# K and V as 8 KB rows, and P and dS turned by VectorE blocks, in a one-core attention and MLP gradient kernel

## The chip, the core and the metric

The kernel runs on one core of one Trainium2 chip. Its time is the device time of one execution in microseconds. The engines are named as the profile names them: PE is TensorE (PEld its weight loads), DVE is VectorE, ACT is ScalarE, POOL is GpSimd, SP is SyncE. Transfers issued by SP run on queue q1, those issued by POOL on queue q0; both are served by the same 16 DMA engines of the core.

## The reference

One decode step of a transformer block (attention and a gated MLP side by side on a normalised input) and its gradients. Cut to what matters:

```
xn = layernorm(x)                                  # x: [4, 1, 512]
q  = (xn @ wq) -> [4 batches, 32 heads, 128]
k, v = last 1024 of 4096 cache rows, 8 key heads, each shared by 4 query heads
p  = softmax(q k^T / sqrt(128));  o = p v
out = x + o @ wo + (gelu(xn @ w_gate) * (xn @ w_up)) @ w_down
results: out and the gradients by x, k_cache, v_cache, wq, wo, w_gate, w_up, w_down
```

All tensors are bf16. The gradients by k_cache and v_cache have the full shape [4, 8, 4096, 128]; the first 3072 rows of each head are zeros and are written as zeros. With them, each execution writes 81 MB and reads 31 MB.

## The kernel before

The kernel has four stages. The MLP stage (to about 60 us in the profiled execution) computes the MLP forward and backward and the weight gradients dW_down, dW_up and dW_gate. A short stage then forms q and the gradient of the attention output (`do_ps`), spread over masks (`bd`, `rows`, `dyBD`). The attention stage runs over the 4 batches b. The end stage forms out, dx, dW_o and dW_q.

In each batch, `scores(0, b)` forms S from q and K, and `scores(1, b)` forms dP from the output gradient and V. Each does four DVE transposes of 128 x 1024 uint32 into a scratch tile `scr` (two buffers) and 8 PE products per transpose, with 32 weight columns and 256 moving columns. `softmax` gives P; `turned` turns P so that keys lie on partitions; `odq(0, b)` multiplies P by V; `spread` and `dvdk(0, b)` form dV; `softmax_d` gives dS; then `turned`, `odq(1, b)` (dq, reads K) and `dvdk(1, b)` (dK). A `dvdk` makes 16 PSUM banks (`kv_ps`), each copied by `evac` into one of four staging tiles `stg`, and stores two tiles of 1 MB.

K and V of a batch are 2 MB each. A tile holds 128 partitions x 8 heads x 8 key rows x 128; partition m has key rows 8m to 8m+7 of every head, so that a run in memory is 2 KB. `load_kv` loads it as two transfers of 1 MB. V has one buffer (`va`), K two (`ka`, `kb`). K of batch 0 is issued by SP, all other K and V by POOL, as are all result stores (`result`). POOL issues in one order with its copies and memsets.

The zeros are written by SP as 32 transfers of 1.5 MB from `ztile` with rows of 12 KB from every second partition (`zeros`). At most three are in flight, and most are tied to an event: two or more follow the landing of each load of K or V, the last ones follow a softmax, an `odq` or an eviction. They fill the transfers' time between loads and stores.

A planner orders the instructions of each engine other than SP from costs; `evac` picks ACT or DVE by running totals (`load`). What sets the order of POOL's transfers before is this planner.

In `turned`, 32 PE products with P (or dS) as weights and a 32-column selection `selp` as the moving operand write one PSUM bank, and one copy evicts it:

```
for j in range(J):
    for a, q in enumerate(quad):
        mm(ps[q, j, :], src[:, j * Q:(j + 1) * Q], selp[:, a].rearrange("p c r -> p (c r)"), pos=(0, Q * a))
pT = att.tile([P, J, Q], BF16, name="pT", tag=f"pT{k}")
evac(pT[:], ps[:], NJ)
```

Of the kernel before, what the change touches and what calls it, by code (L numbers as in the profile page):

```python
# [8 lines left out]
ACT = mybir.ActivationFunctionType  # L9
# [9 lines left out]
def kernel(  # L19
# [71 lines left out]
    def t32(out, in_, n):  # L91
        load["dve"] += (130 + n) / 0.96
        nc.vector.transpose(out=out, in_=in_)  # L93
# [17 lines left out]

    def result(out, in_):
        return store(nc.gpsimd, out, in_, "rest", ["zeros", "rest"], single_packet=True)

    def mm(out, lhsT, rhs, first=True, last=True, pos=None):
        kw = {} if pos is None else {"tile_position": pos}
        nc.tensor.matmul(out, lhsT=lhsT, rhs=rhs, start=first, stop=last, **kw)  # L117
# [42 lines left out]
    def mask(name, n, in_):  # L160
# [10 lines left out]
    omt = const.tile([P, NQ, 2], FP32, name="omt")  # L171
    TT(out=omt[:], in0=gmask[:].rearrange("p (c g) -> p c g", g=2), in1=bm[:].unsqueeze(2).broadcast_to([P, NQ, 2]),
       op=ALU.mult)
    om = mask("om", 2, omt[:].rearrange("p c g -> p g c"))
    oms = const.tile([P, 2], FP32, name="oms")
    TS(out=oms[:], in0=om[:], scalar1=scale, scalar2=None, op0=ALU.mult)
# [7 lines left out]
    selp = const.tile([P, 4, NQ, 8], BF16, name="selp")  # L184
    for a in range(4):
        TS(out=selp[:, a], in0=rs2[:, :, 0, :], scalar1=amask[:, a:a + 1], scalar2=None, op0=ALU.mult)
# [26 lines left out]
    dyBD = const.tile([P, NPB, 2, P], BF16, name="dyBD")  # L213
    nc.gpsimd.memset(dyBD[:], 0.0)
# [12 lines left out]
    def load_kv(b, k, pool, tag, eng, **kw):  # L227
        d_, src = ((k_t, A_k_cache), (v_t, A_v_cache))[k]
        tl = pool.tile([P, G, J, Dh], BF16, name=tag, tag=tag)
        for hf in range(2):  # L230
            hs = slice(hf * G // 2, (hf + 1) * G // 2)
            with tc.high_priority():
                d = eng.dma_start(out=tl[:, hs].rearrange("p g j d -> p g (j d)"),  # L233
                                  in_=src[b, hs, K0:Sk, :].rearrange("g (m j) d -> m g (j d)", j=J), **kw)
# [25 lines left out]
    if True:  # L260
# [85 lines left out]
        for wi, (wsb, dh, og) in enumerate(((wu_sb, dhu, out_7), (wg_sb, dhg, out_6))):  # L346
# [26 lines left out]
            for h in range(2):  # L373
# [7 lines left out]
                result(dwg_v[h], stg[:, 0:2 * F])  # L381
# [3 lines left out]
    with tc.tile_pool(name="mid", bufs=1, reuse_waits="tile") as mid:  # L385
# [4 lines left out]
        with tc.tile_pool(name="att", bufs=1, reuse_waits="tile") as att:  # L390
            zeros(2, load_kv(0, 1, att, "va", nc.gpsimd, single_packet=True))
            zeros(3, load_kv(1, 0, att, "kb", nc.gpsimd, single_packet=True))

# [4 lines left out]
            for k in range(2):  # L398
                bd.append([])
                for u in range(2):  # L400
                    t_ = att.tile([P, DPB, NQ, 2, 2, Q], BF16, name=f"bd{k}{u}")
                    nc.gpsimd.memset(t_[:], 0.0)
                    bd[k].append(t_)
# [65 lines left out]

            spread_rows(1, get_d)  # L470
# [9 lines left out]

            def scores(k, b):
# [4 lines left out]
                for g2 in range(2):  # L486
                    for e in range(2):
                        sc = scratch()
                        t32(sc[:].rearrange("p (c j m) -> p c j m", c=NQ, j=J), src[:, g2:G:2, :, e * Q:(e + 1) * Q], 1024)
                        sb = sc[:].bitcast(BF16).rearrange("p (c n r) -> p c r n", c=NQ, r=2)  # L490
# [15 lines left out]
            def turned(src, k):  # L506

                ps = bank("pT_ps", "x", (P, J, Q))
                for j in range(J):
                    for a, q in enumerate(quad):  # L510
                        mm(ps[q, j, :], src[:, j * Q:(j + 1) * Q], selp[:, a].rearrange("p c r -> p (c r)"), pos=(0, Q * a))
                pT = att.tile([P, J, Q], BF16, name="pT", tag=f"pT{k}")
                evac(pT[:], ps[:], NJ)
# [32 lines left out]
            def softmax_d(P_f, dP):  # L546
# [9 lines left out]
                STT(out=dS_b[:], in0=dP, scalar=cc[:, 0:1], in1=P_f[:], op0=ALU.subtract, op1=ALU.mult)  # L556
                load["dve"] += 1200
                return dS_b

            def dvdk(k, b, sp, r_):  # L560
# [4 lines left out]
                for j in range(0, J, 2):  # L565
                    ps = [bank("kv_ps", "w", (P, 2, 2, Dh)) for _ in range(NQ)]
                    for u in range(2):
                        for c, q in enumerate(quad):
                            mm(ps[c][:, u].rearrange("p g d -> p (g d)"), sp[q, j + u].rearrange("p a m -> p (a m)"),
# [208 lines left out]
```

## Time and profile before

| what | value |
|---|---|
| median of 3 runs | 282.73 us (281.98 to 283.4) |
| the profiled execution | 282.91 us, its span 280.8 us |
| busy in the span | PE 67%, DVE 58%, ACT 44%, POOL 21% |
| queue q1 (SP) | 66.46 MB, 57.0% of 16 engines |
| queue q0 (POOL) | 45.35 MB, 41.5% of 16 engines |
| moved | 112.21 MB, mean 400 GB/s |
| granted PE clock | mean 0.581 |

The span runs from the first to the last instruction; 2.1 us of the time lie outside it. The share of a queue is the time that its packets took, over 16 engines for the span. The attention stage begins at about 76 us and its last store is issued at 241.8 us.

### The profile page before, as it was taken

To read this page: it belongs to the slowest core of one execution; us is meant where nothing else is said; L and a number is where in the kernel's file an instruction comes from. 1 tells how busy PE (TensorE), PEld (TensorE's weight loads), DVE (VectorE), ACT (ScalarE), POOL (GpSimd) and SP (SyncE) were. 2 spreads that over 40 slices of the span, in tenths; PEclk is the share of its full clock that TensorE was granted. 3 is DMA by queue.
4 is the path that set the end of the run, shared out by engine and by line. 5 is a ranking of instruction groups with operands and counts; after the bars stand their busy time and mean duration, and the time that the engine had idled before them with its cause. 6 is when DMAs were issued, how large, how long until landed. Compare 5 with 4: busy or idle time off the path is not lost.

```text
span 280.8 us, 4407 instructions
## 1 busy us (share of the span) xinstructions
PE 187.0 (67%) x1733; PEld 76.1 (27%) x1733; DVE 162.9 (58%) x309; ACT 124.3 (44%) x245; POOL 60.2 (21%) x135
## 2 busy tenths in 40 slices
PE   0318899859444899659956642963357998955870
PEld 0102354233122623224321321321034232511210
DVE  2879656898796525545128350474496104397870
ACT  1133764730100569634824402722441768445870
POOL 8500110169083314130040060020020020201110
PEclk9975955558955556655555555555555555685555
DMA  7999999999999999999999999999999999999995
GB/s 246 427 443 443 388 396 420 425 426 411 389 427 434 420 356 403 308 373 415 424 412 407 421 427 409 371 428 427 436 373 418 415 408 402 390 411 386 414 412 242
DMA packets 17027, 112.21 MB, mean 400 GB/s; under 512 B 1384, under 2 KB 1648, under 8 KB 11376
## 3 DMA queue, kind: packets, MB, share of 16 engines
q1 hardware_dynamic: 6688, 66.46, 57.0%
q0 software_dynamic: 10176, 45.35, 41.5%
q8 instruction: 13, 0.21, 0.3%
q10 hardware_dynamic: 144, 0.13, 0.1%
q14 instruction: 6, 0.05, 0.0%
HBM read 30.93 MB, written 81.01 MB: 399 GB/s over the span
## 4 chain that ended last, share of the span: by engine, by line
PE 25%; DMA 24%; DVE 13%; issue 4%; ACT 4%; POOL 1%; POOLq 0%; DVEq 0%; ACTq 0%
DMA out_dram<-stg 16%; PE kv_ps L117 9%; DVE scr L93 6%; DMA ka<-in_A_k_cache_dram 5%; PE sc_ps L117 3%; ACT stg L88 3%; DMA kb<-in_A_k_cache_dram 3%; PE od_ps L117 3%; PE ok_ps L117 2%; PE ob_ps L117 2%; DVE stg L89 2%; DVE wq_sb L93 2%; PE dxq_ps L117 2%; PE dwq_ps L117 1%; PE dwo_ps L117 1%
## 5 line engine op out<-in xcount | busy, mean ns | idle before, releaser
L88 ACT CAST stg<-kv_ps 128x512 bf16<-128x512 f32 x118 | 63.7, 606 | 56.1 <-DMA out_dram<-stg 28.1
L106 POOL DMA_DIRECT2D out_dram<-stg x30 | 19.7, 659 | 146.3 <-ACT stg L88 96.1
L117 PE MATMUL sc_ps<-scr,bd 128*32 128x256 bf16 x256 | 24.2, 395 | 21.2 <-DVE scr L93 17.9
L117 PE MATMUL kv_ps<-dm,spr 32*128 32x256 bf16 x128 | 28.8, 400 | 6.7 <-ACT stg L88 5.1
L117 PE MATMUL kv_ps<-qm,spr 32*128 32x256 bf16 x128 | 24.9, 385 | 11.0 <-ACT stg L88 10.5
L93 DVE STREAM_TRANSPOSE scr<-va 128x1024 uint32<-128x1024 uint32 x16 | 18.8, 1217 | 10.9 <-DMA va<-in_A_v_cache_dram 10.9
L117 PEld LDWEIGHTS <-spr 32*128 32x128 bf16 x256 | 12.3, 102 | 46.3 <-issue 42.0
L117 PEld LDWEIGHTS <-bd 128*32 128x32 bf16 x256 | 8.1, 107 | 33.4 <-issue 32.7
L88 ACT CAST stg<-dwg_ps 128x448 bf16<-128x448 f32 x26 | 12.7, 552 | 6.7 <-PE dwg_ps L117 5.8
L88 ACT CAST stg<-dwo_ps 128x512 bf16<-128x512 f32 x18 | 10.0, 588 | 10.1 <-PE dwo_ps L117 9.9
L117 PE MATMUL dwo_ps<-dy_b,oSP 32*128 32x512 bf16 x32 | 9.0, 516 | 6.6 <-ACT stg L88 5.2
L89 DVE CAST stg<-kv_ps 128x512 bf16<-128x512 f32 x10 | 6.6, 679 | 11.8 <-DMA out_dram<-stg 6.3
L93 DVE STREAM_TRANSPOSE scr<-ka 128x1024 uint32<-128x1024 uint32 x8 | 9.6, 1227 | 5.4 <-DMA ka<-in_A_k_cache_dram 3.3
L93 DVE STREAM_TRANSPOSE scr<-kb 128x1024 uint32<-128x1024 uint32 x8 | 9.8, 1232 | 5.0 <-DMA kb<-in_A_k_cache_dram 4.4
L233 POOL DMA_DIRECT2D va<-in_A_v_cache_dram x8 | 6.0, 756 | 30.9 <-PE od_ps L117 27.1
L588 DVE SCALAR_TENSOR_TENSOR odt<-od_ps,oms,odt 128x128 f32<-128x128 f32 x4 | 1.4, 340 | 18.0 <-ACT odt L587 18.0
L117 PE MATMUL do_ps<-scr,dyBD 128*128 128x512 bf16 x32 | 10.1, 454 | 2.3 <-DVE scr L93 2.1
L117 PE MATMUL dwq_ps<-dqSP,xn_b 32*128 32x512 bf16 x32 | 10.6, 587 | 1.1 <-ACT stg L88 0.4
L89 DVE CAST stg<-dwq_ps 128x512 bf16<-128x512 f32 x15 | 9.9, 688 | 1.8 <-PE dwq_ps L117 1.6
L117 PEld LDWEIGHTS <-pT 128*32 128x32 bf16 x256 | 9.2, 140 | 5.2 <-ACT pT L88 2.3
L88 ACT CAST stg<-dwq_ps 128x512 bf16<-128x512 f32 x17 | 9.6, 586 | 1.6 <-PE dwq_ps L117 0.9
L89 DVE CAST stg<-dwo_ps 128x512 bf16<-128x512 f32 x14 | 9.2, 679 | 1.9 <-PE dwo_ps L117 1.6
(196 smaller groups left out, 321.1 us busy)
## 6 DMA issues: line engine op xcount, KB each, us to landing
out_dram<-ztile SPq DMA_DIRECT2D x32, 1536.0 KB, 12.2
out_dram<-stg POOLq DMA_DIRECT2D x24, 1024.0 KB, 10.7
va<-in_A_v_cache_dram POOLq DMA_DIRECT2D x8, 1024.0 KB, 15.0
out_dram<-stg POOLq DMA_DIRECT2D x6, 896.0 KB, 10.8
wq_sb<-in_A_wq_dram SPq DMA_DIRECT2D x1, 4096.0 KB, 24.0
wo_sb<-in_A_wo_dram SPq DMA_DIRECT2D x1, 4096.0 KB, 34.2
kb<-in_A_k_cache_dram POOLq DMA_DIRECT2D x4, 1024.0 KB, 19.4
ka<-in_A_k_cache_dram SPq DMA_DIRECT2D x2, 1024.0 KB, 42.2
```

The costliest lines, as they stand in the source:

```text
L88: return nc.scalar.copy(out=out, in_=in_)
L89: return nc.vector.tensor_copy(out=out, in_=in_)
L93: nc.vector.transpose(out=out, in_=in_)
L106: d = eng.dma_start(out=out, in_=in_, **kw)
L117: nc.tensor.matmul(out, lhsT=lhsT, rhs=rhs, start=first, stop=last, **kw)
L233: d = eng.dma_start(out=tl[:, hs].rearrange("p g j d -> p g (j d)"), in_=src[b, hs, K0:Sk, :].rearrange("g (m j) d -> m g (j d)", j=J), **kw)
L588: done = STT(out=t_[:], in0=ps[:, 1, :], scalar=mk[:, 1:2], in1=t_[:], op0=ALU.mult, op1=ALU.add)
```

## The change

Four things change together.

1. K and V tiles become [128, 2, 32, 128]: partition 4m+c holds key rows 32m to 32m+31 of heads 2c and 2c+1, so that a run in memory is 8 KB. A load is four transfers of 512 KB, one for each c, each writing every fourth partition. In `scores`, the DVE transposes read this layout, and the products' moving operand picks its 256 columns out of `scr` with steps of 1 KB, 16 B and 128 B, where it had a step of 4 B.
2. `turned` transposes P or dS by 32 x 32 blocks on DVE, does 16 PE products with a constant selection (`sel4`) as weights and 64 moving columns, and evicts the bank in four parts, each with a per-partition mask (`pmask`) and all 256 columns, two on DVE and two on ACT. `odq` then has, as weights, slices of this tile with zeros where the partition is of another c.
3. POOL's transfers get a fixed order, that of the program (`in_order`). The last store of the MLP stage is written after the first loads of V and K. `later` adds order without a wait: the first products of `dvdk` come after the last of `odq`, and the transposes of wq are placed in the last batch.
4. The two masks of dP (`bd[1]`) lie in the memory of `dyBD`, which is cleared by a POOL memset after `do_ps`.

```
     def load_kv(b, k, pool, tag, eng, **kw):
         d_, src = ((k_t, A_k_cache), (v_t, A_v_cache))[k]
-        tl = pool.tile([P, G, J, Dh], BF16, name=tag, tag=tag)
-        for hf in range(2):
-            hs = slice(hf * G // 2, (hf + 1) * G // 2)
+        tl = pool.tile([P, 2, Q, Dh], BF16, name=tag, tag=tag)
+        row = tl[:].ap[0][0]
+        for c in range(NQ):
             with tc.high_priority():
-                d = eng.dma_start(out=tl[:, hs].rearrange("p g j d -> p g (j d)"),
-                                  in_=src[b, hs, K0:Sk, :].rearrange("g (m j) d -> m g (j d)", j=J), **kw)
+                d = eng.dma_start(out=bass.AP(tensor=tl.tensor, offset=tl.offset + c * row,
+                                              ap=[[NQ * row, Q], [Q * Dh, 2], [1, Q * Dh]]),
+                                  in_=src[b, 2 * c:2 * c + 2, K0:Sk, :].rearrange("g (m j) d -> m g (j d)", j=Q), **kw)
+            if eng is nc.gpsimd:
+                in_order(d)
...
-                    t_ = att.tile([P, DPB, NQ, 2, 2, Q], BF16, name=f"bd{k}{u}")
-                    nc.gpsimd.memset(t_[:], 0.0)
-                    bd[k].append(t_)
+                    if k == 0:
+                        t_ = att.tile([P, DPB * NQ * 4 * Q], BF16, name=f"bd{u}")[:]
+                        nc.gpsimd.memset(t_, 0.0)
+                    else:
+                        t_ = dyBD_t[:, u * 1024:(u + 1) * 1024]
...
+            nc.gpsimd.memset(dyBD_t[:], 0.0)
             spread_rows(1, get_d)
...
-                        t32(sc[:].rearrange("p (c j m) -> p c j m", c=NQ, j=J), src[:, g2:G:2, :, e * Q:(e + 1) * Q], 1024)
-                        sb = sc[:].bitcast(BF16).rearrange("p (c n r) -> p c r n", c=NQ, r=2)
+                        turned_last[0] = t32(sc[:].rearrange("p (j x) -> p j x", j=Q),
+                                             src[:, g2, :, e * Q:(e + 1) * Q], 1024)
+                        sb = sc[:].bitcast(BF16).rearrange("p (h j m c r) -> p c r j m h", h=4, j=J, m=8, c=NQ)
...
-            def turned(src, k):
-
-                ps = bank("pT_ps", "x", (P, J, Q))
-                for j in range(J):
+            def turned(src):
+
+                T = att.tile([P, J, 4, 8], BF16, name="T", tag="T")
+                t32(T[:].rearrange("p j a r -> p (j a r)"), src[:], NJ)
+                ps = bank("pT_ps", "x", (P, 4, J, 8))
+                for h in range(4):
                     for a, q in enumerate(quad):
-                        mm(ps[q, j, :], src[:, j * Q:(j + 1) * Q], selp[:, a].rearrange("p c r -> p (c r)"), pos=(0, Q * a))
-                pT = att.tile([P, J, Q], BF16, name="pT", tag=f"pT{k}")
-                evac(pT[:], ps[:], NJ)
+                        mm(ps[q, h], sel4[:, h, :], T[:, :, a, :], pos=(0, Q * a))
+                pT = att.tile([P, 4, J, Q], BF16, name="pT", tag="pT")
+                pv = pT[:].rearrange("p h l (c r) -> p (h l) c r", c=NQ)
+                for c in range(NQ):
+                    in_ = ps[:].rearrange("p h l r -> p (h l) r")
+                    if c % 2:
+                        nc.scalar.activation(out=pv[:, :, c], in_=in_, func=ACT.Copy, scale=pmask[:, c:c + 1])
+                    else:
+                        TS(out=pv[:, :, c], in0=in_, scalar1=pmask[:, c:c + 1], scalar2=None, op0=ALU.mult)
```

The compiled order of the changed kernel shows where the pieces fall. In the first batch, DVE's order after the softmax is: the third transpose of the next batch's K, the block transpose `T`, the four `spread` operations, the first masked eviction, the product with dP (`Gt`), the fourth transpose of K, the second masked eviction. PE does 23 score products of the next batch ahead of the 16 of `turned`, and 9 more between these and the `od_ps` products. POOL's order from then on is: V of the next batch (4 transfers), two dV stores, K (4), two dK stores, and so on.

## The prediction

> **What bounds the kernel now.** I read the page's slices first, then the queues' totals, then the queues stretch by stretch, and last the order of the engines where the DMA row dips. First the page: span, DMA row, queues.
>
> ```profile
> span 280.8 us, 4407 instructions
> DMA  7999999999999999999999999999999999999995
> q1 hardware_dynamic: 6688, 66.46, 57.0%
> q0 software_dynamic: 10176, 45.35, 41.5%
> ```
>
> No slice but the first and last is under 90%, and the two queues' packets took 98.5% of the 16 engines' span. No compute engine is over 67%. So bytes, at their price in DMA time, set the end; the change moves the same bytes. It can win by a lower price of a byte or by filling a gap, and lose by a higher price or a new gap. Compute matters only where the transfers run dry.
>
> The price comes from the queue rows of short stretches (packets, MB, share). In order: 71 to 77 us, loads of K and V alone; 150 to 175, zeros (q1) with loads and stores (q0); 253 to 263, stores of 8 KB rows beside zeros; 265 to 274, the same alone; 85 to 95, zeros alone; 110 to 124, loads and stores of 2 KB rows together.
>
> ```profile
> q0 software_dynamic: 599, 2.31, 102.1%
> ...
> q1 hardware_dynamic: 699, 7.73, 73.0%
> q0 software_dynamic: 714, 2.76, 27.5%
> ...
> q0 software_dynamic: 315, 2.29, 56.1%
> ...
> q0 software_dynamic: 511, 3.68, 99.6%
> ...
> q1 hardware_dynamic: 384, 4.23, 99.8%
> ...
> q0 software_dynamic: 927, 3.61, 79.5%
> ```
>
> MB over share times length gives MB per us of the 16 engines. Rows of 2 KB: alone 2.31/6.13 = 0.377, beside zeros 2.76/6.88 = 0.401, in the mixed stretch 3.61/11.1 = 0.324. Rows of 8 KB: alone 3.68/8.96 = 0.411, beside zeros 2.29/5.61 = 0.408. Zeros, 12 KB rows: 4.23/9.98 = 0.424. Bytes over packets tell the grain: 3.9 KB per packet for 2 KB rows, 7.3 KB for 8 KB rows.
>
> The one gap inside the attention stage, by DMA slices of 0.2 us from 98 to 106 us, and what stands before it (VectorE, PE and POOL in order of time):
>
> ```profile
> DMA  9599896998999999998999999998563523396974
> ...
> 91.59 1.25 DVE L93 STREAM_TRANSPOSE scr<-kb 128x1024 uint32<-128x1024 uint32 x1 [0.39 <-PE sc_ps L117]
> 92.76 0.83 DVE L502 TENSOR_SCALAR spr<-P_b,amask 128x256 bf16<-128x256 bf16 x4
> 93.51 0.42 DVE L549 CUSTOM_DVE_ANT_0 Gt<-P_f,sc_ps 128x256 f32<-128x256 f32 x1
> 93.85 1.24 DVE L93 STREAM_TRANSPOSE scr<-kb 128x1024 uint32<-128x1024 uint32 x1
> ...
> 93.09 2.10 PE L117 MATMUL od_ps<-va,pT 128*32 128x256 bf16 x32
> ...
> 95.51 1.50 POOL L233 DMA_DIRECT2D va<-in_A_v_cache_dram  x2 [2.21 <-PE od_ps L117]
> ```
>
> At 95.5 us the second batch's V is asked for, as soon as `od_ps` has read the first. It ends near 104, the next zeros wait for its landing, and the row falls to 2 to 6 tenths for some 1.2 us.
>
> **The change, part by part.** Each term is against the profiled execution: 282.91 us, span 280.8 and 2.1 around it; it stands 0.2 above the median 282.73, so no correction is needed.
>
> *K and V in 8 KB rows.* POOL's 14 loads of 1 MB are 14.68 MB. No load with 8 KB rows is in the trace; the nearest rows are the stores. If all ran alone: 14.68/0.377 = 38.9 us becomes 14.68/0.411 = 35.7, -3.2. If all ran beside zeros: 36.6 becomes 36.0, -0.6. In the stretches above, about two thirds of them run without zeros: -2.4. Outer bounds: -4.3 (0.377 to the zeros' 0.424), and a loss if rows on every fourth partition cost more (rival D). K of the first batch on SP goes at 0.388 (37 to 46 us); 2.1 MB at 0.411 give -0.3. The mixed stretch lost 3.61/0.324 - 3.61/0.377 = 1.5 us more; why, the trace does not show, so a cure is bounded by 0 and -1.5; I take -0.5, as only the load half of its rows changes.
>
> The transfers on POOL rise by 14 and on SP by 2. A POOL issue took 0.75 us for 1 MB in 2 KB rows and 0.53 for 1 MB in 8 KB rows; four of the latter are 2.1 us against 1.5 per load, on an engine that is 21% busy: nothing. In the compiled order a transfer of POOL waits for the eighth before it, and a load now takes four of the eight; since seven are still in flight behind that wait, the queue does not run dry: nothing; bound: the 0.6 us of one issue per load, 4 us in all.
>
> *The turn.* Per batch and direction PE goes from 32 products (0.41 us in a run) to 16 with twice the columns, at least 0.2 less or the same. DVE gains a block transpose of 256 (0.40 us as D3d; upper bound 0.975 for the bf16 448-wide aT) and two evictions of 256 (0.41 each, as the reduction of the same bank): 1.2 us. ACT goes from one copy of 0.40 to two of 0.51 (P_b): +0.6. Eight times: DVE +9.8, ACT +5. Both have cover where transfers bound (DVE 58%, ACT 44%); what is left is the first batch. There, by the compiled order, the third K transpose ends at 92.8 as now, `T` 93.2, `spread` 94.05, first eviction 94.5, `Gt` 94.9, fourth transpose 96.1, second eviction 96.5; 9 score products, the 32 of `od_ps` (1.9), and V is asked for at 99.2 to 99.4 instead of 95.5: 3.8 us late. Behind it in SP's order stand two zeros that wait for its landing, behind it on POOL two dV stores that come as late. What hides it: zeros left in flight. q1 moved 1.60 MB between 95 and 105, 3.8 us at 0.424, so alone they end at 98.8; V's first packets would come near 99.9. The DMA engines stand idle 1.1 us: +1.0. Bounds: 0 (if the planner's order slips forward) and 3.8 (if nothing is in flight).
>
> *Masks of dP in dyBD.* The memset waits for `do_ps` (ends 72.6) and takes 1.8 us; then 1.0 of `selb` and 1.8 of `bd` for q end at 77.2, where the first score product began at 77.1: 0.1 us, inside the DVE's transposes (to 85.9). Nothing; uncovered it would be 2.
>
> *POOL's order.* K of the next batch but one now stands behind both dV stores; in the first batch it was ahead of one. It waits for the evictions, which `od_ps` waits for too (ACT evicts `pT` after the 16 `kv_ps`). Zeros follow later by as much, while two stores (2 MB, 5 us) are in flight: nothing, bound +1.5 (the gap between 109.7 and 111.2).
>
> *Order of wq's transposes and odq.* In the last batch two transposes of 1.21 us now stand ahead of `dqs`; 1.2 of it fits the wait of DVE for dqr (1.19 us). The tail's stores keep the queue full to 276 us: nothing, bound +1.2. V's transposes now stand behind the turn in later batches, so each later V load is asked for some 4 us later than `od_ps` allows; there q0 holds 2 to 6 MB already, 5 us or more. Nothing.
>
> Sum: -2.4 - 0.3 - 0.5 + 1.0 = -2.2; 282.9 - 2.2 = 280.7.
>
> One rule of the Trainium skill weighs against this part: DMA: Bandwidth & Descriptors, section Rules for kernel authors, asks for 128 partitions and at least 1 MiB per transfer, and its section on one DMA's anatomy gives a fixed 2.0 us per transfer. If that were paid in turn, 14 more transfers for the seven POOL loads would cost an estimated 28 us by that page. The trace disagrees for 1 MB pieces: their packets filled 102.1% of a stretch with several in a row; no run here shows 512 KB pieces yet.
>
> **Rivals.** B, no change: the loads mostly share the engines with zeros or keep their price (-0.6), K on SP -0.3, and the late V takes +1.0 with no cure of the mixed stretch: 283.0. For it: 0.401 beside zeros against 0.408.
>
> C, slower, by PE's reads. The moving operand of the 256 score products steps 16 B or more for every column; in the trace it stepped 4 B, and 8 more products cost 0.43 us (16 take 1.05, 8 take 0.62). If a far step makes a product three times as long, 8 take 1.5 us where DVE feeds them every 1.13: the first 64 gain 2.8 us, the 32 of the next K, which stand before `od_ps`, 3.4. V is late by 6 us more in the place above, all of it idle: about 287. It decides from some 2.5 times on (then V is 3.7 us later still, and 280.7 + 3.7 is over 0.5% slower); at twice (1.05 us per 8, under the 1.13) it adds about 2. Against: nothing in the trace steps so far, and half the PE clock (0.50 to 0.53 there) leaves the reads slack. The Trainium skill, Advanced Engine Details and Errata, section Memory Cachelines, says that accesses which each touch another 16-byte line pay a penalty, without a size; no run here shows it yet.
>
> D, slower, by the loads. Rows on every fourth partition, in pieces of 512 KB, fill the engines worse. If 8 KB rows alone cost 1.2 times the old price (0.314 MB per us), the 9.8 MB outside zeros would take 31.2 us instead of 26.0: +5.2, with the late V's 1.0 about 289. It decides from some 1.03 times on: 0.7 us more, with +1.0 for V and -0.3 for K on SP, is 0.5%. Against: zeros leave from every second partition at 0.424. For: they are reads of SBUF, and 1.5 MB each.
>
> E, faster still: the mixed stretch is cured, and loads no longer wait behind zeros at 4 KB against 12 KB a turn, so gaps of the 0.3 us kind elsewhere close: 276.5 to 278.
>
> **How the numbers follow.** Forecast 0.42, its own range 278.5 to 281.6; B 0.22; C 0.10; D 0.16; E 0.10. About 0.5%, 1.4 us, is what a measurement of this kernel can tell from no change; some of the forecast's upper end falls there. Faster 0.48, same 0.26, slower 0.26. The range 276 to 289 leaves out the end of E, and of C and D what lies above: about 0.13.
>
> **What would show it.** Right: q0's packets near 7 KB in stretches of loads, 0.40 or more MB per us there; V of the second batch asked for near 99 and a gap of 1 to 2 us near 99; DMA row at 9 elsewhere. C shows in `sc_ps` runs of 8 over 0.62 us and idle DMA at 95 to 110; D in loads alone under 0.37 MB per us; E in a mean rate over 406 GB/s. Wrong would be a DMA row that runs dry in later batches: then the turn's chain, not the bytes, would set the time there.

## The result and the profile after

The changed kernel takes 293.93 us, the median of 6 runs (293.38 to 295.57), against 282.77 for the kernel before on the same chip: 1.040 times as long, with a 95% interval of 1.037 to 1.044. The forecast was 280.7 with a range of 276 to 289. One run of the experiment called e16 below took 322.1 us, in a slower state, and is left out of its median.

First the page of the changed kernel, the lines that answer to those shown of before: span, DMA row in 40 slices, and the two queues (packets, MB, share of the 16 engines).

```profile
span 293.6 us, 4212 instructions
...
DMA  7999999999999267999999999999999999999982
...
q1 hardware_dynamic: 5952, 66.46, 54.6%
q0 software_dynamic: 8608, 45.35, 39.1%
```

The packets took 54.6 + 39.1 = 93.7% of 293.6 us, 275.1 us; before, it was 98.5% of 280.8, 276.6 us. So all bytes together became cheaper, by 1.5 us. What grew is the time in which the engines had no bytes: 4.2 us of the span before, 18.5 us now. The row shows where: the slices at 95 to 117 us, and the last two.

The DMA row of 95 to 118 us, in slices of 0.575 us:

```profile
DMA  9998311000000000096999978994100599999999
```

From 97.3 us on the row is at 3 and under, and from 99.0 to 104.8 it is empty; by the digits the hole is worth 7.3 us. A second one of some 2.3 us stands at 110.5 to 113.4. Before, there was one of 1.2 us here. The windows of both places (PE, PEld, DVE, ACT, POOL busy, then PE clock, DMA share, GB/s):

```profile
95.00:115.00 20.00, 13.77 (x162) 6.25 (x158) 8.54 (x24) 11.20 (x23) 5.63 (x14) 0.59 0.52 196
265.00:294.00 29.00, 13.38 (x45) 3.04 (x42) 14.39 (x22) 13.47 (x24) 3.20 (x6) 0.50 0.72 298
```

At 95 to 115 the DMA engines stood idle 0.48 x 20 = 9.6 us, and in what is left of the span from 265 on 28.6 - 0.72 x 29 = 7.7 us.

Why V of the second batch is asked for at 103.9 instead of 95.5 us is seen on POOL and DVE (start, length, engine, line, what, and in brackets the idle time before it and what ended that). POOL:

```profile
68.17 0.54 POOL L245 DMA_DIRECT2D kb<-in_A_k_cache_dram  x1 [5.51 <-DMA out_dram<-stg]
70.66 0.55 POOL L106 DMA_DIRECT2D out_dram<-stg  x1 [1.95 <-DMA va<-in_A_v_cache_dram]
71.19 1.86 POOL L421 MEMSET bd<- 128x1024 bf16 x2
...
75.16 1.80 POOL L491 MEMSET dyBD<- 128x2048 bf16 x1
...
103.87 2.13 POOL L245 DMA_DIRECT2D va<-in_A_v_cache_dram  x4 [0.88 <-PE od_ps L129]
```

(`x2`, `x3` and `x4` count instructions in a row.) The fourth quarter of `kb` waits 5.51 us, because a transfer of POOL waits for the eighth before it (here a dW store; counted back along POOL's issues, the transfer named in the brackets is the eighth); the last dW store behind it waits 1.95 more, for V's first quarter. Behind both stand the memsets, which now start at 71.2 instead of 62.2. They fall beside DVE's preparation of dO. DVE:

```profile
74.20 0.83 DVE L480 CAST scr<-hm 128x128 bf16<-128x128 f32 x1
...
75.02 2.65 DVE L484 TENSOR_SCALAR scr<-scr,d4mask 128x128 bf16<-128x128 f32 x4
...
97.18 0.40 DVE L93 STREAM_TRANSPOSE T<-P_b 128x256 bf16<-128x256 bf16 x1
...
98.71 0.48 DVE L546 TENSOR_SCALAR pT<-pT_ps,pmask 128x256 bf16<-128x256 f32 x1 [0.38 <-PE pT_ps L129]
...
99.45 1.24 DVE L93 STREAM_TRANSPOSE scr<-kb 128x1024 uint32<-128x1024 uint32 x1
100.61 0.44 DVE L546 TENSOR_SCALAR pT<-pT_ps,pmask 128x256 bf16<-128x256 f32 x1
```

The two casts into `scr` took 0.19 and 0.22 us before and the four `d4mask` instructions 1.04; now 0.83, 0.80 and 2.65. K's first score products start at 81.5 instead of 77.1. The last four lines are the turn: `T` at 97.18, first eviction of `pT` at 98.71, then K's fourth transpose, and the second eviction at 100.61. PE starts `od_ps` at 101.64; before, at 93.09. And each score product takes longer (minimum, median, maximum in ns of the 128 products of S; the 256 of before had a median of 396):

```profile
L129 PE MATMUL sc_ps<-scr,bd x128: 614/636/680, 81.5 to 201.9; 128*32 128x256 bf16 x128
```

The end stage, POOL's stores of dwo and dwq, the gradients dW_o and dW_q (the first three and the last; before, the first came at 252.03, the third at 258.89, the last at 273.67):

```profile
254.61 0.55 POOL L106 DMA_DIRECT2D out_dram<-stg  x1 [8.91 <-DVE stg L89]
259.96 0.55 POOL L106 DMA_DIRECT2D out_dram<-stg  x1 [4.80 <-ACT stg L88]
268.71 0.53 POOL L106 DMA_DIRECT2D out_dram<-stg  x1 [8.20 <-DVE stg L89]
271.69 0.53 POOL L106 DMA_DIRECT2D out_dram<-stg  x1 [2.44 <-ACT stg L88]
...
284.31 0.53 POOL L106 DMA_DIRECT2D out_dram<-stg  x1 [2.46 <-issue]
```

The first comes 2.6 us later than before; the third waits 8.20 us for a staging tile. From 271.7 on a store leaves every 3.2 us, while its 1.05 MB take the DMA engines 2.5 us at 0.42 MB per us, so their share is 0.85 to 0.89 from 272 to 286 us.

These lines also divide the loss. The profiled span is 12.8 us longer than before: 2.6 us up to dwo's first store, 8.1 between the first store and the last (29.7 us against 21.6), and 2.2 behind the last (9.3 against 7.1). So most of the loss shows only in the end stage; e2 below ties it to the early hole.

### The profile page after: what moved, and what is told of

Same layout as the page of the kernel before. It is cut to its first block, busy times and chain, and to the rows that moved or that the text cites. A ratio compares the mean times of both kernels' runs of the same rounds, so it can differ in the third digit from the quotient of the medians.

```text
span 293.6 us, 4212 instructions
## 1 busy us (share of the span) xinstructions
PE 188.4 (64%) x1603; PEld 71.6 (24%) x1605; DVE 173.3 (59%) x327; ACT 128.9 (44%) x258; POOL 65.2 (22%) x148
## 3 DMA queue, kind: packets, MB, share of 16 engines
q1 hardware_dynamic: 5952, 66.46, 54.6%
q0 software_dynamic: 8608, 45.35, 39.1%
## 4 chain that ended last, share of the span: by engine, by line
PE 29%; DMA 19%; DVE 17%; issue 16%; ACT 13%; POOL 1%; SPq 1%; POOLq 0%; DVEq 0%; ACTq 0%
DMA out_dram<-stg 11%; ACT stg L88 9%; DVE scr L93 7%; PE sc_ps L129 7%; DMA va<-in_A_v_cache_dram 5%; DMA wu_sb<-in_B_w_up_dram 4%; PE dwg_ps L129 3%; PE od_ps L129 3%; PE kv_ps L129 3%; PE do_ps L129 2%; PE da_ps L129 2%; PE q_ps L129 2%; PE dwq_ps L129 1%; ACT pT L544 1%; DVE stg L89 1%
## 5 line engine op out<-in xcount | busy, mean ns | idle before, releaser
L129 PE MATMUL sc_ps<-scr,bd 128*32 128x256 bf16 x128 | 20.6, 636 | 13.1 <-DVE scr L93 13.1
L129 PE MATMUL kv_ps<-dm,spr 32*128 32x256 bf16 x128 | 21.3, 333 | 2.0 <-ACT stg L88 1.3
L129 PEld LDWEIGHTS <-spr 32*128 32x128 bf16 x256 | 11.2, 101 | 34.7 <-issue 32.2
L129 PE MATMUL sc_ps<-scr,dyBD 128*32 128x256 bf16 x128 | 18.9, 636 | 0.5 <-DVE scr L93 0.4
L546 DVE TENSOR_SCALAR pT<-pT_ps,pmask 128x256 bf16<-128x256 f32 x16 | 7.7, 480 | 17.4 <-ACT pT L544 14.7
L129 PE MATMUL dwo_ps<-dy_b,oSP 32*128 32x512 bf16 x32 | 8.9, 524 | 12.5 <-ACT stg L88 12.3
L129 PEld LDWEIGHTS <-pT 128*32 128x32 bf16 x256 | 10.4, 134 | 24.0 <-ACT pT L544 20.2
L544 ACT ACTIVATE pT<-pT_ps,pmask 128x256 bf16<-128x256 f32 x16 | 8.0, 499 | 15.0 <-DVE pT L546 15.0
L129 PE MATMUL od_ps<-va,pT 128*32 128x256 bf16 x128 | 10.0, 412 | 6.8 <-ACT pT L544 6.8
L129 PEld LDWEIGHTS <-dyBD 128*32 128x32 bf16 (+1 forms) x176 | 9.6, 112 | 18.1 <-issue 14.4
L245 POOL DMA_DIRECT2D va<-in_A_v_cache_dram x16 | 8.6, 541 | 22.8 <-issue 18.1
```

The costliest lines, as they stand in the source:

```text
L129: return nc.tensor.matmul(out, lhsT=lhsT, rhs=rhs, start=first, stop=last, **kw)
L245: d = eng.dma_start(out=bass.AP(tensor=tl.tensor, offset=tl.offset + c * row, ap=[[NQ * row, Q], [Q * Dh, 2], [1, Q * Dh]]), in_=src[b, 2 ...
L544: nc.scalar.activation(out=pv[:, :, c], in_=in_, func=ACT.Copy, scale=pmask[:, c:c + 1])
L546: TS(out=pv[:, :, c], in0=in_, scalar1=pmask[:, c:c + 1], scalar2=None, op0=ALU.mult)
```

## The experiments

All times are medians, with the kernel before, measured beside each, at 282.66 to 283.15 us; ratios are to it, with 95% intervals. "V asked" is the first transfer of the second batch's V on POOL, "dwo" the issue of dwo's first store, both from the profiled run. The diffs below are shortened; a line of words in them stands for several lines of code. In e1, e3, e9 and e10 the keys stand in another order than the rest of the kernel takes them to, so these four compute with other keys; the amount of work is the same.

```
run                      us       ratio [interval]         V asked   dwo
before                   282.8                              95.5     252.0
after                    293.9    1.040 [1.037, 1.044]     103.9     254.6
e1  loads alone          295.3    1.043 [1.038, 1.048]      99.6     261.5
e9  loads + order        290.0    1.025 [1.022, 1.029]      99.3     249.8
e10 e9 + memsets first   287.1    1.017 [1.012, 1.022]      96.7     242.2
e2  zeros ahead          286.9    1.014 [1.012, 1.016]     103.9     254.0
e3  near reads           292.5    1.034 [1.031, 1.037]     102.3     247.1
e4  turn first           288.7    1.022 [1.017, 1.027]     100.9     255.4
e5  memsets first        292.1    1.030 [1.022, 1.037]     101.8     252.2
e6  e5 + own mask        291.9    1.033 [1.028, 1.037]     102.3     252.0
e11 e2 + e4 + e6         287.3    1.014 [1.008, 1.019]      99.7     255.4
e12 e11, one zero ahead  287.1    1.012 [1.005, 1.019]     100.2     255.9
e14 far step in DVE      302.8    1.070 [1.065, 1.075]     110.7     270.4
e15 e12 + e14            301.9    1.065 [1.060, 1.069]     105.9     269.8
e16 e2, wq earlier       289.5    1.021 [1.015, 1.026]     102.7     256.6
e17 e2, end free         287.2    1.014 [1.008, 1.019]     104.1     257.4
e18 e11, end free        296.7    1.049 [1.044, 1.054]      98.1     263.9
e19 before, zero ahead   284.2    1.004 [1.002, 1.007]      95.0     253.6
e20 e2, dK free          288.0    1.015 [1.009, 1.020]     104.2     251.7
e21 e20, wq behind dqs   288.0    1.018 [1.013, 1.023]     103.9     252.3
```

The theory at the start: the loss is DMA time left idle by the late V, not dearer bytes. The rivals: the loads in this form are dearer; or the idle engines only show a chain of compute that sets the end anyway.

### What the gap costs (e2)

```diff
-            zeros(3, load_kv(1, 0, att, "kb", ...))
+            zeros(5, load_kv(1, 0, att, "kb", ...))
 (last batch)
-                    zeros(2, o_done)      # twice
+                    zeros(1, o_done)
```

> The changed kernel, with two transfers of zeros (3.1 MB) moved from the last batch (3, 2, 2 become 3, 1, 1) to behind the first load of K on POOL (3 become 5). Theory (what costs is the 7.3 us in which the DMA engines had nothing, 97.5 to 104.8): two zeros fill 3.1/0.424 = 7.4 us there, the time falls by 5 to 7 us to 287 to 289, V of the second batch is asked for at 104 as before. Rival (the chain of compute sets the end, the idle DMA engines only show it): 293 to 295, and the 7 us turn up as idle DMA later.

Measured 286.9, 7.0 us under the changed kernel, with V asked for at 103.86 as there. Row of 95 to 118, and the windows:

```profile
DMA  9899989998999999898896999998000499999999
```

```profile
95.00:115.00 20.00, 13.73 (x158) 6.22 (x157) 8.60 (x24) 11.19 (x23) 5.62 (x14) 0.59 0.89 356
235.00:265.00 30.00, 23.22 (x203) 7.39 (x199) 20.45 (x40) 19.37 (x39) 3.67 (x6) 0.61 0.92 369
265.00:285.00 20.00, 8.62 (x27) 2.00 (x26) 9.15 (x14) 8.73 (x16) 2.14 (x5) 0.50 0.77 314
```

The 7.3 us hole is gone and the time with it, nearly one for one: the gap is the largest single cause. V is as late as ever, so lateness by itself did not cost; having no bytes to move did. This run also takes two zeros away from dwo's stores, which alone could help the end; but e3, e5 and e6 below leave the zeros where they are, and there too the time follows the idle time of 95 to 115 us: it is 1.2, 2.4 and 2.0 us less than in the changed kernel (shares 0.58, 0.64 and 0.62), and the times are 1.4, 1.9 and 2.0 us less. Some 4 us against before remain in e2, now as idle DMA engines behind 235 us (shares 0.92 and 0.77).

### What makes V late (e3 to e6)

e3 lets the score products read in steps of 4 B; the scores' key columns come out in another order.

```diff
-  sb = ....rearrange("p (h j m c r) -> p c r j m h", h=4, j=J, m=8, c=NQ)
+  sb = ....rearrange("p (c n r) -> p c r n", c=NQ, r=2)
```

> The changed kernel, with the score products reading their moving operand in steps of 4 B as before the change; the keys' columns come out in another order, so the scores meet other keys. Theory: 8 products take 0.62 us again instead of 1.03 to 1.15, each group of 8 ends 0.4 to 0.5 us earlier, V of the second batch is asked for 2 to 3 us earlier (101 to 102), and the time falls by 2 to 3 us, to 291 to 292. Rival (DVE, which makes a group in 1.2 us, sets the pace, and the far reads hide under it): V is asked for at most 0.6 us earlier, the time stays within 1 us of 293.9.

```profile
L129 PE MATMUL sc_ps<-scr,bd x128: 369/396/418, 81.5 to 195.2; 128*32 128x256 bf16 x128
```

The products fall from 636 to 396 ns, V is asked for at 102.31, 1.56 us earlier, and the time falls by 1.4 us. Both were below what the theory expected: the 8 products of a block take 1.03 to 1.15 us, and DVE's 1.2 us per block hides most of that.

e4 puts DVE's turn ahead of the rest of the batch.

```diff
+  if k == 0 and g2 == 1 and moved_last[0] is not None:
+      later(turned_last[0], moved_last[0])     # K's 3rd and 4th transpose
+  (the same for spread's four masks and for Gt)
```

> The changed kernel, with the third and fourth block transpose of the next K, the four masks of spread and Gt placed behind DVE's second eviction of pT, in every batch. Theory (V of the second batch is late by what DVE and PE do between P_b and od_ps): the third transpose, its 8 products, spread, Gt and the fourth transpose leave that stretch, V is asked for 3 to 4 us earlier (100 to 101), the time falls by 2.5 to 4 us to 290 to 291.5. Rival (the work only moves behind and delays dV's stores and the second batch's scores by as much): 293 to 295.

```profile
95.18 0.45 DVE L93 STREAM_TRANSPOSE T<-P_b 128x256 bf16<-128x256 bf16 x1 [0.66 <-ACT P_b L579]
96.54 0.48 DVE L549 TENSOR_SCALAR pT<-pT_ps,pmask 128x256 bf16<-128x256 f32 x1 [0.92 <-PE pT_ps L129]
97.63 0.48 DVE L549 TENSOR_SCALAR pT<-pT_ps,pmask 128x256 bf16<-128x256 f32 x1 [0.60 <-ACT pT L547]
98.03 0.86 DVE L530 TENSOR_SCALAR spr<-P_b,amask 128x256 bf16<-128x256 bf16 x4
```

`T` to the second eviction now takes 2.9 us (95.18 to 98.11) instead of 3.9; V comes 3.0 us earlier and the time falls by 5.3 us, more than expected: the share of 95 to 115 rose from 0.52 to 0.69, which is 3.4 us, and the rest shows at the end, where the third store of dwo waits 3.87 us for a staging tile instead of 8.20.

e5 and e6 take the memsets off the critical place: first ahead of the quarter at which POOL waits, then also with the first dP mask in memory of its own.

```diff
+  D3, bd, selh, selb, dqs: memsets emitted ahead of load_kv(1, 0)
+  if c == NQ - 1 and pool_clear: later(d, pool_clear.pop())   # quarter 4 behind dqs
   (e6)
-                    if k == 0:
+                    if k == 0 or u == 0:       # bd10 has its own tile
```

> The changed kernel, with POOL's memsets of the q masks, selh and dqs placed ahead of the last quarter of K of the second batch, the transfer at which POOL waited 5.5 us for the eighth before it; the memset of dyBD stays where it was. Theory (POOL's wait and its late memsets make the first scores late): memsets from 63 instead of 71.2, of 4.4 us of lateness at the first scores some 2 go (the memset of dyBD still runs beside DVE's casts), V of the second batch is asked for at 101.5 to 102.5 instead of 103.9, time 291 to 292.5. Rival (the lateness comes from the memset of dyBD beside DVE alone): V at 103.5 or later, time 293 to 294.5.

> As the run with the memsets first, and with the first batch's mask of dP in its own memory, set to zero among the early memsets; only the second mask stays in dyBD and is set to zero (1024 columns) after the first masks are filled. Theory (POOL's memset at 72 to 77 makes DVE's casts and masks of dO, 0.19 and 1.04 us before, take 0.83 and 2.65): these come back to their old lengths, the first scores start at 77 to 78, V is asked for at 99.5 to 100.5, time 289 to 291. Rival (those instructions are slow for another reason): as the run with the memsets first, 291 to 292.5.

DVE's instructions in e5 and in e6:

```profile
74.91 0.90 DVE L482 CAST scr<-hm 128x128 bf16<-128x128 f32 x1
...
75.79 1.08 DVE L486 TENSOR_SCALAR scr<-scr,d4mask 128x128 bf16<-128x128 f32 x4
```

```profile
74.96 0.18 DVE L482 CAST scr<-hm 128x128 bf16<-128x128 f32 x1
...
75.19 1.05 DVE L486 TENSOR_SCALAR scr<-scr,d4mask 128x128 bf16<-128x128 f32 x4
```

In e5, with only the dyBD memset left beside DVE, the casts are still slow and the masks fast; in e6, with none beside it, all are at their old lengths. So POOL's memset beside DVE is what lengthened them. In time it is little: e5 came as expected, with V 2.1 us earlier and 1.9 us gained; e6 brought nothing more (V 1.6 us earlier than in the changed kernel, 2.0 us gained), and its rival, that it would be as e5, was the better forecast of its time. The first scores of e6:

```profile
L129 PE MATMUL sc_ps<-scr,bd x192: 614/636/682, 79.9 to 199.8; 128*32 128x256 bf16 x192
```

They start at 79.9, not at the expected 77 to 78. So of the 4.4 us by which the first scores are late, the memsets are 1.6, or 2.4 if one counts that the transposes of `do_ps` start 0.8 later in e6 than in the changed kernel (73.72 and 72.96; before 72.60). In e6, too, K's first transpose stands behind `D3d` and `dm`.

### The loads by themselves (e1, e9, e10)

The kernel before with the changed `load_kv` alone; then with POOL's order by hand (`in_order`, `last_dw`); then with the memsets first.

```diff
-        for hf in range(2):  # 1 MB, 2 KB rows
+        for c in range(NQ):  # 512 KB, 8 KB rows on partitions c, c + 4, ...
```

> The kernel before, with the loads of K and V alone taken from the change (8 KB rows on every fourth partition, four transfers of 512 KB each); everything else, the masks and POOL's free order too, stays. The rows lie in another order than the rest of the kernel assumes, so K, V and what follows from them are those of other keys. Theory (the bytes got cheaper, the loss is DMA time left idle by the turn and by POOL's late memsets): packets' time falls by 1.5 to 3 us and the time with it, to 280 to 281.5; some of it can be lost again because POOL stands at the eighth transfer before its memsets (up to 2 us). Rival (loads in this form are dearer, or disturb the zeros): 284 or more, with loads alone under 0.377 MB per us.

```profile
99.64 1.59 POOL L233 DMA_DIRECT2D va<-in_A_v_cache_dram  x3 [2.21 <-PE od_ps L117]
111.72 1.60 POOL L233 DMA_DIRECT2D ka<-in_A_k_cache_dram  x3 [10.50 <-PE od_ps L117]
113.32 0.53 POOL L233 DMA_DIRECT2D va<-in_A_v_cache_dram  x1
```

295.3: the loads alone, without the turn, cost 12.5 us, where the theory had expected a gain. The price of bytes, the rival's reason, was not it: the loads alone (69 to 75 us) moved 2.52/(1.001 x 6) = 0.420 MB per us, and all packets took (54.5 + 39.6)% of 294.6 = 277.2 us. In POOL's free order the quarters of V and K are mixed: V's fourth is issued 13.7 us after the first three, behind K's, and everything that needs V, and the zeros that follow it, waits.

> The kernel before, with the loads in four transfers of 8 KB rows and POOL's transfers in the order written by hand; the turn, the score products' reads and the masks of before stay (K and V are those of other keys, as in the run of the loads alone). Theory (the loads alone cost 12 us because the quarters of several loads were mixed on POOL and waited for the eighth before them; in order, they cost nothing): no gaps near 128 and 235 us, only the late memsets are left (V of the second batch at 99 to 100), 282 to 285. Rival (more and smaller transfers on POOL cost as much in any order): 290 or more.

> As the run of loads and order, with POOL's memsets ahead of the last quarter of K of the second batch. Theory: V of the second batch is asked for at 95 to 96.5 as in the kernel before, no gap at 98 to 105, and the cheaper bytes (1.5 to 2 us of packets' time) come through: 280 to 282. Rival (the loads' price is not lower once nothing runs dry): 282.5 to 284.

The order by hand takes 5.3 us off; still, e9's theory (282 to 285) failed, and its 290.0 is the rival's value. The early memsets take off 2.9 more. V is then asked for at 96.7, 1.2 us later than before the change, and packets take (56.1 + 40.1)% of 285.3 = 274.5 us, 2.1 less than before; yet the time is 287.1, so e10's theory failed. Its row of 92 to 112 us in slices of 0.5, and POOL's loads:

```profile
DMA  9999998999749899798998940000299999999998
```

```profile
96.68 2.13 POOL L242 DMA_DIRECT2D va<-in_A_v_cache_dram  x4 [2.21 <-PE od_ps L126]
...
136.55 0.55 POOL L242 DMA_DIRECT2D kb<-in_A_k_cache_dram  x1 [2.43 <-DMA out_dram<-stg]
140.12 0.53 POOL L242 DMA_DIRECT2D kb<-in_A_k_cache_dram  x1 [3.01 <-DMA va<-in_A_v_cache_dram]
143.62 0.54 POOL L242 DMA_DIRECT2D kb<-in_A_k_cache_dram  x1 [2.97 <-DMA va<-in_A_v_cache_dram]
```

By the row V has landed by 104, and the next zeros are issued at 105.8, so 2.7 us are empty, against 1.2 before. Later each quarter of `kb` waits some 3 us for the eighth transfer before it. The end stage starts early here (dwo at 242.2) and takes 34.9 us to its last store instead of 21.6: staging tiles come free late, beside the zeros.

### All mends together (e11, e12)

> The changed kernel with the mends together: POOL's memsets ahead of the last quarter of K and the first mask of dP in its own memory, DVE's turn ahead of the next K's last two transposes, spread and Gt, and two transfers of zeros moved ahead. Theory (the loss is DMA time left idle, first by the late V, then in the last 50 us because the chain of compute comes late): V of the second batch is asked for at 98 to 99.5, the row stays at 9 there but for 2 us, the last stage starts 4 us or more earlier, 281.5 to 284. Rival (the last stage, evictions at 3 us per MB and staging tiles held by slow stores, keeps the 6.5 us of idle that it has with the zeros moved alone): 284.5 to 286.

> As the run of all mends, with one transfer of zeros moved ahead instead of two. Theory: with V asked for at 98 to 99.5, one zero (3.7 us) fills what is left of the gap, and the other does more at the end, where the DMA engines wait for evictions: 0.5 to 1.5 us less than with two, 281 to 283.5. Rival (the end doesn't take it: the stores are held up behind zeros there): the same as with two or more.

Measured 287.3 and 287.1. e11 is slower than its rival had it too (284.5 to 286); e12 is as its rival said, the same as e11. The windows of e11:

```profile
95.00:115.00 20.00, 13.92 (x159) 6.56 (x151) 8.02 (x22) 12.19 (x25) 6.28 (x14) 0.50 0.98 402
235.00:265.00 30.00, 22.97 (x211) 7.62 (x204) 20.69 (x39) 19.48 (x39) 3.15 (x5) 0.61 0.79 319
265.00:286.00 21.00, 10.10 (x32) 2.21 (x29) 10.41 (x16) 10.13 (x18) 2.67 (x5) 0.50 0.79 321
```

The row is full at 95 to 115 (0.98), and the idle time has moved to the end: 6.3 us from 235 to 265 and 4.2 behind. dwo's first store at 255.4 was 3.4 us later than before. With one zero less ahead (e12), 3.0 us more of gap cost nothing. So once the gap is small, more bytes ahead no longer help, and e2 is already at that floor.

### The far step moved to DVE (e14, e15)

```diff
-  t32(sc[:].rearrange("p (j x) -> p j x", j=Q), ...)
+  t32(sc[:].rearrange("p (c j m h) -> p h j m c", c=NQ, j=J, m=8), ...)
```

> The changed kernel, with the far step moved from PE's read to DVE's write: the block transposes of K and V write their blocks so that the score products read in steps of 4 B, in the right order of keys. Theory (PE reads far steps at half speed, DVE writes at its own pace): 8 products take 0.62 us, the transposes stay at 1.25 us, and the time is that of the run with near reads in the wrong order, 291.5 to 293. Rival (DVE's writes pay for the far step as PE's reads did): the transposes take 2 us or more, V of the second batch is asked for 5 us later or more, 298 or more.

> The run with all mends and one transfer of zeros moved ahead, with the far step in DVE's writes. Theory: as the run with all mends and one zero, less 0.5 to 1.5 us, 280 to 283. Rival: if DVE's transposes get dearer, 290 or more.

```profile
L93 DVE STREAM_TRANSPOSE scr<-va 128x1024 uint32<-128x1024 uint32 x16 | 30.2, 2009 | 0.0
```

A block transpose that writes in far steps takes 2.0 us instead of 1.23; the products are at 402 ns. V comes at 110.7, and the time is 302.8 (301.9 with the mends, 14.7 over e12). Both rivals came true: PE was the cheaper place for the far step.

### The end (e16 to e21)

e16 to e18 change the order in the last batch, on e2 or e11:

```diff
   (e16)  later(wq_done[k], ds_done)            # k = 4..7, for 6 and 7 was o_done
   (e17, e18)  no later() for wq; and
-                            if j == u == 0:
+                            if j == u == 0 and (k, b) != (1, B - 1):
                                 later(p_, od_last)
   (e20)  only this last diff;  (e21)  and o_done taken behind the copies to dqs
```

> The changed kernel with two zeros moved ahead, and in the last batch the last two block transposes of wq no longer between od_ps and dqs, but before dS's turn with the two before them. Theory (with the gap filled, the chain of compute in the last 30 us sets the end, and these two transposes, 2.3 us, lie in it where only 1.2 fit the wait for dqr): the first store of dwo is issued 1 to 1.3 us earlier (252.8 to 253.1 instead of 254.0), the time is 285.6 to 286.2. Rival (the end is set by transfers, as it was before the change): 286.5 to 287.5.

In e16 `d`, DVE's transpose ahead of `dqs`, came 0.4 us earlier than in e2 (235.68, 236.10) but `oSP`, which dwo's products read, 2.1 later (246.24, 244.17). 18 of dK's products then took turns on PE with those of dxq, where it was 12 in e2, and the copy `okT`, behind dK's evictions on ACT, came 2.1 us later. The time, 289.5, is above what theory and rival gave: the step that I suspected does not pay by itself.

> As the changed kernel with two zeros moved ahead, but without both of the change's orders for wq's transposes, and with the last batch's dK products free to go ahead of od_ps as before the change. Theory: dK's evictions start before od_ps, dqs comes right behind dqr, dwo's first store is issued at 251 to 252.5 as before the change (252.0), the time is 283.5 to 285. Rival (the wq transposes, 9.3 us, now hold up the last K's transposes, or the end is set by transfers): 286.5 or more.

> As the run with all mends and two zeros moved ahead, with the end freed in the same way. Theory: it had dwo's first store at 255.4 and 10 us of idle DMA engines behind 235; the end comes 2 to 4 us earlier, 283 to 285.5. Rival: its first V at 100 no longer matters and the time is that of the run with the end free and without those mends, 283.5 to 287.

e17 was as e2, e18 far worse than theory and rival: free of their orders, the eight transposes of wq go ahead of the last K's (9.3 us on DVE), and dwo starts at 257.4 and 263.9. In e18 DVE's last eviction of `pT` also waits 7.74 us for ACT's, which stands behind evictions of `kv_ps`. Freeing wq and dK together did not pay; e20 frees dK alone.

> The changed kernel with two zeros moved ahead, and the last batch's dK products no longer held behind od_ps: 12 of 32 go ahead of it, in the 2.2 us in which PE waits for the evictions of pT. Theory (the order of dK behind od_ps lengthens the last chain, because PE does dK between dqs and dwo): od_ps as late as before or 0.5 us later, dwo's first store at 251.5 to 253 instead of 254.0, time 285 to 286. Rival (the end is set by transfers): 286.5 to 287.5.

> The run with dK free, and the last two block transposes of wq behind the four copies of dqs instead of ahead of them. Theory: dqs comes 1.1 us earlier (only 1.2 of the 2.3 us fit the wait for dqr), dwo's first store at 250.5 to 252, as early as in the kernel before (252.0), time 284 to 285.5. Rival: the copies come earlier but PE has dK to do, time as the run with dK free alone.

Here the theory's step came as expected and its result did not: dwo's first store at 251.7 and 252.3, as in the kernel before, but 288.0 in both, for e20 above its rival's range too. e20's stores:

```profile
251.70 0.55 POOL L106 DMA_DIRECT2D out_dram<-stg  x1 [9.41 <-DVE stg L89]
256.09 0.55 POOL L106 DMA_DIRECT2D out_dram<-stg  x1 [3.84 <-ACT stg L88]
261.14 0.53 POOL L106 DMA_DIRECT2D out_dram<-stg  x1 [4.50 <-DVE stg L89]
...
276.62 0.53 POOL L106 DMA_DIRECT2D out_dram<-stg  x1 [2.51 <-issue]
```

From the first store to the last it takes 24.9 us, against 21.6 in e2 and before: the third waits 4.5 us for a staging tile.

> The kernel before, with one transfer of zeros moved from the last batch to behind the first load of K on POOL, as two were in the changed kernel. Theory (a gap costs what it is long): its gap at 104 us is 1.2 us, the time falls by 0.5 to 1.2 us to 281.5 to 282.2. Rival (the end then lacks the zeros and its compute sets the time): 282.5 to 284.

The row of 235 to 275 us:

```profile
DMA  9999986999998999400399799899799998999999
```

The gap at 104 us is closed (share of 95 to 115 is 1.01), and the time is 0.4% longer: idle time stands at 251 to 255 us instead, and dwo starts 1.5 us later. So in the kernel before, too, the end is not set by bytes alone.

## Why the prediction was wrong, step by step

**"So bytes, at their price in DMA time, set the end."** Half right. In the changed kernel the 7.3 us without bytes cost 7.0 (e2). But e19 filled a hole of the kernel before, e11 and e12 what e2 had left, and none gained. That the chain of compute that ends in dwo stands close behind the bytes, in the kernel before too, is the reading that fits; no run shows the size of its slack. The step took a DMA share of 98.5% as proof that compute had slack.

**"K and V in 8 KB rows": -2.4, with -0.3 and -0.5.** The direction was right; 1.5 us less packets' time in place of 3.2. Loads alone now show, for 69 to 75 us,

```profile
q0 software_dynamic: 389, 2.54, 100.8%
```

which is 2.54/(1.008 x 6) = 0.420 MB per us, above the 0.411 that I took. So rival D fell. The Trainium skill, DMA: Bandwidth & Descriptors, Rules for kernel authors, asks for 128 partitions and at least 1 MiB per DMA for the most bandwidth; here pieces of 512 KB on 32 partitions, queued one behind another, cost no more per byte than the 1 MB stores in 8 KB rows. E fell too: the mean rate was 382 GB/s where it asked for over 406, and transfers of q0 in a mixed stretch (125 to 135 us) still moved at 3.24/(0.952 x 10) = 0.340 MB per us, against 0.324 before.

**"Four of the latter are 2.1 us against 1.5 per load ... nothing; bound: 4 us in all."** This is the step that failed most. I asked whether the queue would run dry behind the wait for the eighth transfer, and not what stands behind it on POOL. There stood the memsets, 9 us late, and with them the masks of the first scores. Loads and order alone cost 7.3 us (e9 against before), 2.9 of them by the memsets (e10): more than my bound, although the bytes did get cheaper. The 4.4 us that e10 still loses are seen in its gap at 104 us and in its long end stage; what causes them stays open.

**"Masks of dP in dyBD ... nothing; uncovered it would be 2."** The cover was gone, since everything on POOL ran late; the neighbours on DVE took 0.64, 0.58 and 1.61 us longer. They were held rather than slowed, by their ends: in the changed kernel the memset of dqs ends at 74.95 and the casts at 75.03 and 75.10, the memset of dyBD at 76.96 and the four masks at 77.67, three mask lengths later; in e5 the dyBD memset ends at 75.72 and the casts at 75.81. The Trainium skill, SBUF — State Buffer, Who interferes with whom, has it so: one of the two engines gets a shared pair of ports for its whole instruction and the other blocks fully. The rows agree. That the memset costs is right (e6 against e5: DVE back at its old lengths), but by then the times of e5 and e6 lie 0.2 us apart, which their runs cannot tell from nothing.

**"The turn ... V is asked for at 99.2 to 99.4 ... 1.1 us: +1.0."** The mechanism and the place were right, the size was not: V at 103.9, and the zeros in flight out near 97.5, not 98.8. Of the 8.4 us, 4.4 are the late first scores (1.6 to 2.4 of it the two steps above, by e6; K's first transpose now stands behind D3d and dm in DVE's order) and 4 the turn, for which I had counted 3.8. In the sum this is the term that was furthest off: +1.0, where filling the hole gave back 7.0 (e2). Inside the turn I had DVE and ACT evict side by side; the trace has them one behind the other, each `pT` eviction waiting for the one before it on the other engine. The bound "3.8 (if nothing is in flight)" fell because it held the lateness of the turn alone. Of the 8.4 us the zeros in flight cover some 2 (the hole grew from 1.2 to 7.3 us); what exceeds them was paid in full.

**Rival C** was right in mechanism: far steps make a product 636/396 = 1.6 times as long, 8 take 1.03 to 1.15 us against 0.62, and "at twice it adds about 2": 1.4 us (e3). So the slack that I expected of half a PE clock was not there. The Trainium skill, Advanced Engine Details and Errata, Memory Cachelines, has a penalty for accesses that each touch another 16-byte line; the rows agree with it and give a size, though no run shows that this is the reason. Rival C did not decide.

**"Order of wq's transposes and odq ... nothing, bound +1.2."** Not settled. In e2 the two transposes do stand between `odt` and `dqs` (2.3 us, where DVE waited 1.19 before), but neither moving them (e16) nor freeing dK as well (e21) shortened the time.

**POOL's order, "nothing, bound +1.5".** Wrong in sign: with loads in quarters, free order mixes them, and the loads alone cost 12.5 instead of 7.3 us (e1, e9).

What stays open is the last 4 us between e2 and the kernel before. In the profiled runs they are 3.7 us: dwo's first store comes 2.0 us later (254.04 for 252.03), the stores take 21.6 us in both, and behind the last one stand 8.9 us instead of 7.1. Shown is that the DMA engines stand idle 3.7 us longer behind 235 us (6.5 against 2.8), that two runs with dwo as early as before the change (e20, e21) did not win them, that three with dwo earlier still (e3, e9 and e10, at 247.1, 249.8 and 242.2) ended later than the kernel before, and that one with the early gap closed (e11) did not win them either. Argued, not shown, is that the end needs both an early dwo and no backlog of stores and zeros beside it. None of the versions beat the kernel before.

## What to carry to other kernels

A queue that is nearly full does not mean that compute is free: move one transfer of filler into a hole, and see whether the time follows, before pricing anything by bytes alone. Splitting a transfer can cost by the instructions that stand behind it on the issuing engine, because its wait for an earlier transfer holds them all (5.5 and 1.95 us here); put what others need soon ahead of the piece that waits. Where a large load can only be asked for after a read, count everything between on every engine, from the start of the stage, and compare it with the bytes in flight: what exceeded them was paid nearly one for one here.

## What was unexpected of the hardware

- A memset of 128 x 2048 on POOL (1.8 us) held fp32-to-bf16 casts, and another the first of four tensor-scalar masks, on DVE until it ended (casts 0.19 to 0.83 us, four masks 1.04 to 2.65); which of DVE's instructions are exempt the runs do not show.
- Steps of 16 B, 128 B and 1 KB in the moving operand, instead of 4 B, made PE's products 1.6 times as long (396 to 636 ns for 256 columns); block transposes on DVE that wrote in far steps took 1.6 times as long as well (1.23 to 2.0 us).
- Quarters of 512 KB, queued one behind another, moved at 0.420 MB per us, as fast as the zeros in 12 KB rows (0.424).
